# Attention sums and values in four column strips, DMA transposes from the eleventh pair on, and a new division of the first batch, in a fused attention and MLP kernel

## The chip, the cores and the metric

The kernel runs on one core of a Trainium2 chip. The metric is device time in microseconds, the median of the runs shown. Lower is better.

## The reference, cut to what matters

Cosine attention over 8 batches of 12 heads (448 positions, 64 dimensions each), and behind it an MLP with a leaky ReLU on the 3584 tokens that come out.

```
q, k, v: (8, 12, 448, 64) f32, tau = 0.1
q_n = q / (norm(q) + 1e-6);  k_n = k / (norm(k) + 1e-6)
attn = softmax(q_n @ k_n.T / tau)
x = (attn @ v), laid out as (8 * 448, 12 * 64) = (3584, 768)
h = x @ w_in                        # w_in (768, 2048)
out = max(0.01 * h, h) @ w_out      # w_out (2048, 768)
```

## The kernel before, in words

The work is cut into 48 slots, one for each pair of heads (8 batches of 6 pairs, `NSLOT`). A pair's 448 positions lie as 112 partitions of 4 positions (`P`, `T4`). For each pair:

- `load` (L73) brings q, k and v by three DMAs of 224 KB on SP's queue. `squares` (L90, on POOL in the loop), `sums` (L101, DVE), `roots` (L107, ACT: a logarithm and an exponential), `recips` and `normalise` (L111, L120, DVE) make the normalised q and k as bf16 tiles `qn`. `cast_v` (L83, POOL) makes the bf16 v.
- `transposes` (L135) turns `qn` by 8 TensorE transposes into one PSUM tile `tp`, and one copy on DVE brings them to `qkT`, with the 64 dimensions of the two heads on 128 partitions.
- `scores` (L153) makes key-by-query scores for the key blocks that it is given, two of four at a time; each of the two heads takes 64 rows of the array, and ACT takes the exponential of both heads' scores in one instruction (L170), into `pe`. There are two score tiles `sc` in PSUM.
- `values` (L176) sums the exponentials by a matmul with `ones` (`sm`, L181), takes the reciprocal on ACT as Exp(-Ln) (`rb`, L188 and L189), and multiplies with v (`po`, L193). Head 0 has output partitions 0 to 63 and head 1 has 64 to 127: two strips of 64 columns. `scale_out` (L201) multiplies `po` by `rb` on DVE, into `xT`, which holds two batches with the 768 model dimensions on partitions.

The MLP runs in 8 chunks of 384 or 512 tokens (`chunk_cols`). `first` (L217) makes one block of 128 hidden units from 6 matmuls (L223), with a Prelu on ACT (L229) to `hT`. `second` (L233) makes 128 tokens by 384 outputs from 16 matmuls (L237), a copy on DVE (L246) and output DMAs on SP's queue (L257). The tiles `tp`, `sm`, `po` and the MLP's `pm` and `po2` share four PSUM banks (`p_mm`).

The order on each engine is the order in which the program issues (`manual_schedule`). Slot s prepares the squares of s + 3, the sums of s + 2 and the transposes of s + 1. In slots 0 to 6 (`EARLY`) there is attention alone; from slot 7 on, `feed` puts MLP groups between the two halves of the scores and behind the second half, by a credit of `MOE_US` = 6.1 us of estimated TensorE time for each slot. A chunk may start in slot 6(c + 1) + 1. The weights come by DMAs from POOL: four of 768 KB for w_in in slots 1 to 4, two of 1536 KB for w_out in slots 5 and 6. Behind slot 48 the rest of the MLP runs by itself.

Of the kernel before, what the change touches and what calls it, by code (L numbers as in the profile page):

```python
# [8 lines left out]
F32 = mybir.dt.float32  # L9
BF16 = mybir.dt.bfloat16  # L10
AF = mybir.ActivationFunctionType
ALU = mybir.AluOpType
# [4 lines left out]
def kernel(  # L17
# [10 lines left out]
    nc = tc.nc  # L28
    B, H, S, D = q.shape
    N_tok, D_model = out.shape  # L30
    D_ff = moe_w_in.shape[1]
# [6 lines left out]
    NSLOT = B * NPAIR  # L38
    KT = D_model // 128
    MT = D_ff // 128  # L40
    HALF = D_model // 2

# [3 lines left out]
    vbp = ctx.enter_context(tc.tile_pool(name="vb", bufs=4))  # L46
# [3 lines left out]
    qtp = ctx.enter_context(tc.tile_pool(name="qt", bufs=2))  # L50
    pep = ctx.enter_context(tc.tile_pool(name="pe", bufs=2))
# [8 lines left out]
    nc.scalar.preload_act_table_set("natural_log_exp_and_others")  # L60
    w_in_sb = cpool.tile([128, KT, D_ff], BF16, name="w_in_sb")
    w_out_sb = cpool.tile([128, MT, D_model], BF16, name="w_out_sb")
    w_in_r = moe_w_in.rearrange("(ko ki) n -> ki ko n", ki=128)
    w_out_r = moe_w_out.rearrange("(mo mi) n -> mi mo n", mi=128)


    def heads(x, s, n):
        b, h0 = s // NPAIR, 2 * (s % NPAIR)
        return x[b, h0 : h0 + 2 * n].rearrange("h (p t) d -> p h t d", t=T4)
# [3 lines left out]
    def load(s, engs=(nc.sync, nc.sync)):  # L73
        raw[s] = []
        for x, eng, name in zip((q, k), engs, ("q_h", "k_h")):
            t = ldp.tile([P, 2, T4, D], F32, name=name)
            eng.dma_start(out=t, in_=heads(x, s, 1))
            raw[s].append(t)
        t = ldp.tile([P, 2, T4, D], F32, name="v_h")
        nc.sync.dma_start(out=t, in_=heads(v, s, 1))  # L80
        vf[s] = t

    def cast_v(s, eng):  # L83
        t = vbp.tile([P, 2, T4, D], BF16, name="v_b")
        eng.tensor_copy(out=t, in_=vf[s])  # L85
        vh[s] = t
# [3 lines left out]
    def squares(s, engs):  # L90
        tiles = []
        for x, eng in zip(raw[s], engs):
            sq = sqp.tile([P, 2, T4, D], F32, name="sq")
            if eng is nc.scalar:
                nc.scalar.activation(sq, x, func=AF.Square)
            else:
                eng.tensor_tensor(sq, x, x, op=ALU.mult)  # L97
            tiles.append(sq)
        sqs[s] = tiles

    def sums(s):  # L101
        x = smp.tile([P, 2, 2, T4], F32, name="ss")
        for i, sq in enumerate(sqs[s]):
            nc.vector.tensor_reduce(x[:, i], sq, axis=AX.X, op=ALU.add)  # L104
        ss[s] = x

    def roots(s):  # L107
        nc.scalar.activation(ss[s], ss[s], func=AF.Ln, bias=tiny)
        nc.scalar.activation(ss[s], ss[s], func=AF.Exp, scale=0.5)

    def recips(s):  # L111

        r = smp.tile([P, 2, 2, T4], F32, name="r")
        nc.vector.tensor_scalar_add(ss[s], ss[s], 1e-6)
        nc.vector.reciprocal(r, ss[s])
        rn[s] = r

    qn = {}

    def normalise(s):  # L120
        pair = []
        for i, x in enumerate(raw[s]):
            t = qnp.tile([P, T4, 2, D], BF16, name=f"qn{i}")
            nc.vector.tensor_tensor(  # L124
                t,
                x.rearrange("p h t d -> p t h d"),
                rn[s][:, i].rearrange("p h t -> p t h").unsqueeze(3).to_broadcast([P, T4, 2, D]),
                op=ALU.mult,
            )
            pair.append(t)  # L130
        qn[s] = pair
# [3 lines left out]
    def transposes(s, copy=nc.vector.tensor_copy):  # L135
        tp = mmp.tile([128, 2, T4, P], BF16, name="tp", tag="mm")
        for i in range(2):
            for t in range(T4):
                nc.tensor.matmul(  # L139
                    out=tp[:, i, t, :],  # L140
                    lhsT=qn[s][i][:, t].rearrange("p h d -> p (h d)"),
                    rhs=id128[:P, :P],
                    is_transpose=True,
                    start=(i == 0 and t == 0),
                    stop=(i == 1 and t == T4 - 1),
                )
        dst = qtp.tile([128, 2, S], BF16, name="qkT")
        copy(out=dst, in_=tp.rearrange("p i t c -> p i (t c)"))  # L148
        qkT[s] = dst
# [3 lines left out]
    def scores(s, kis):  # L153
        if s not in pe:
            pe[s] = pep.tile([P, T4, 2, S], BF16, name="pe")
# [18 lines left out]
    xT, rbs, pos = {}, {}, {}  # L174

    def values(s):  # L176

        sm = mmp.tile([128, 512], F32, name="sm", tag="mm")
        for ki in range(T4):
            for a in range(2):  # L180
                nc.tensor.matmul(  # L181
                    out=sm[64 * a : 64 * a + 64, :S],
                    lhsT=ones,
                    rhs=pe[s][:, ki, a, :],
                    start=(ki == 0), stop=(ki == T4 - 1),
                )
        rb = rbp.tile([128, S], F32, name="rb")
        nc.scalar.activation(rb, sm[:, :S], func=AF.Ln)  # L188
        nc.scalar.activation(rb, rb, func=AF.Exp, scale=-1.0)  # L189
        po = mmp.tile([128, 512], F32, name="po", tag="mm")  # L190
        for ki in range(T4):
            for a in range(2):
                nc.tensor.matmul(  # L193
                    out=po[64 * a : 64 * a + 64, :S],
                    lhsT=vh[s][:, a, ki, :],
                    rhs=pe[s][:, ki, a, :],
                    start=(ki == 0), stop=(ki == T4 - 1),
                )
        rbs[s], pos[s] = rb, po

    def scale_out(s):  # L201
        b, j = divmod(s, NPAIR)
        m, half = divmod(b, 2)
        if m not in xT:
            xT[m] = xtp.tile([128, NPAIR, 2 * S], BF16, name="xT")
        nc.vector.tensor_tensor(  # L206
            xT[m][:, j, half * S : (half + 1) * S], pos[s][:, :S], rbs[s], op=ALU.mult
        )

# [53 lines left out]

    work = []
    for c in range(B):
        c0, n = chunk_cols(c)
        at = NPAIR * (c + 1) + 1
        for m in range(MT):
            work.append((at, 6 * n / 2400, lambda c=c, m=m: first(c, m)))
        for ts in range(n // 128):  # L270
            for half in range(2):
                work.append((at, 16 * HALF / 2400, lambda c=c, ts=ts, half=half: second(c, ts, half)))
    credit = [0.0]

    def feed(slot, us):
        if not work or work[0][0] > slot:
            return
        credit[0] += us
        while work and work[0][0] <= slot and credit[0] >= work[0][1] / 2:
            at, cost, fn = work.pop(0)  # L280
            fn()
            credit[0] -= cost


    def load_w_in(i):
        n0 = i * (D_ff // 4)
        nc.gpsimd.dma_start(
            out=w_in_sb[:, :, n0 : n0 + D_ff // 4], in_=w_in_r[:, :, n0 : n0 + D_ff // 4]
        )

    def load_w_out(i):
        m0 = i * (MT // 2)
        nc.gpsimd.dma_start(
            out=w_out_sb[:, m0 : m0 + MT // 2], in_=w_out_r[:, m0 : m0 + MT // 2]
        )

    gp = nc.gpsimd
# [6 lines left out]
    ones = cpool.tile([P, 64], BF16, name="ones")  # L304
# [6 lines left out]
    recips(0)  # L311
# [3 lines left out]
    cast_v(0, gp)  # L315
# [3 lines left out]
    recips(1)  # L319
    normalise(1)  # L320

    MOE_US = 6.1
    EARLY = 7
    for s in range(NSLOT + 1):
        if s + 3 < NSLOT:
            squares(s + 3, (gp, gp))
        if s + 1 < NSLOT:
            cast_v(s + 1, gp)
        if 1 <= s <= 4:
            load_w_in(s - 1)  # L330
        if 5 <= s <= 6:
            load_w_out(s - 5)
        if s + 4 < NSLOT:
            load(s + 4)
        if s < NSLOT:
            scores(s, (0, 1))
        if s + 2 < NSLOT:
            sums(s + 2)
        if s < EARLY:
            roots(s + 2)  # L340
            transposes(s + 1)
            recips(s + 2)
            if s >= 1:
                values(s - 1)
            scores(s, (2, 3))
            normalise(s + 2)
            if s >= 1:
                scale_out(s - 1)
        else:
            values(s - 1)  # L350
            scale_out(s - 1)
            if s + 2 < NSLOT:
                roots(s + 2)
                recips(s + 2)
            feed(s, MOE_US / 2)
            if s + 1 < NSLOT:
                transposes(s + 1)
            if s < NSLOT:
                scores(s, (2, 3))
            if s + 2 < NSLOT:  # L360
                normalise(s + 2)
        if s >= EARLY:
            feed(s, MOE_US / 2)
    while work:
        feed(NSLOT + NPAIR, 1e9)
# [35 lines left out]
```

## Time and profile before

| | |
|---|---|
| three runs | 487.48, 489.21, 491.65 us; median 489.21 |
| span of the profiled execution | 488.5 us |
| TensorE matmul (PE) busy | 457.7 us, 94% |
| ScalarE (ACT) busy | 300.8 us, 62% |
| VectorE (DVE) busy | 241.1 us, 49% |
| GpSimd (POOL) busy | 139.2 us, 28% |
| DMA | 50.86 MB, mean 104 GB/s |
| mean granted TensorE clock | 0.990 |

The span is the time from the first to the last instruction of one execution on the core, and the busy times are shares of it. Matmuls are pipelined, so a busy PE is not one at its peak. The slices of a row ("tenths") are 40 equal parts of the span, some 12.2 us each. In a line of a group, the last numbers are busy time and mean length of one instruction, then the idle time before them and what ended most of it. SP is the engine whose queue issues most DMAs.

### The profile page before, as it was taken

The numbers are of one execution on the slowest core, as the hardware profiler recorded it, in microseconds if no ns is written. First come the engines' busy times: TensorE is split into PE (matmuls) and PEld (weight loads), VectorE is DVE, ScalarE is ACT, GpSimd is POOL, SyncE is SP. The second block draws the span as 40 slices with busy tenths as digits, with TensorE's granted clock in tenths as the row PEclk, the third lists the DMA queues.
The fourth block names the chain that finished last, engine by engine and source line by source line (L and its number), as shares of the span: only waits on it lengthen the run. The fifth ranks groups of instructions, "written<-read, shape, count | busy, mean of one in ns | idle before, by whom it ended". The sixth has DMA issues, their size and how long they took to land.

```text
span 488.5 us, 8163 instructions
## 1 busy us (share of the span) xinstructions
PE 457.7 (94%) x3186; PEld 240.2 (49%) x3200; DVE 241.1 (49%) x442; ACT 300.8 (62%) x517; POOL 139.2 (28%) x152
## 2 busy tenths in 40 slices
PE   1777899989999999999999999998999999999996
PEld 0333455534445555554455555554445555554463
DVE  4998534573545753474446454456345654120011
ACT  3788776477774578457765467647874558543400
POOL 2976342053230542054222322143222230000000
PEclk9999899989999999999999999999999999999999
DMA  9999990463213460337103551146221330021022
GB/s 195 218 236 244 239 229 7 120 174 85 63 54 92 118 180 23 86 94 203 56 2 103 165 146 58 44 136 191 68 58 34 105 106 2 0 66 32 1 58 72
DMA packets 44455, 50.86 MB, mean 104 GB/s; under 512 B 3329, under 2 KB 40961, under 8 KB 44417
## 3 DMA queue, kind: packets, MB, share of 16 engines
q1 hardware_dynamic: 38960, 43.82, 33.5%
q0 software_dynamic: 5216, 6.29, 7.3%
q8 instruction: 25, 0.41, 0.4%
q10 hardware_dynamic: 240, 0.23, 0.1%
q14 instruction: 14, 0.11, 0.1%
HBM read 45.61 MB, written 11.01 MB: 116 GB/s over the span
## 4 chain that ended last, share of the span: by engine, by line
PE 88%; DMA 5%; ACT 3%; DVE 2%; issue 1%; POOL 1%; SPq 0%; POOLq 0%
PE pm L223 31%; PE po L237 31%; PE sc L162 9%; PE sm L181 8%; PE po L193 7%; PE tp L139 3%; DMA q_h<-in_q_dram 3%; ACT pe L170 2%; DMA v_h<-in_v_dram 2%; DVE qn L124 1%; DVE ss L104 0%; POOL sq L97 0%; ACT rb L189 0%; ACT rb L188 0%; DVE xT L206 0%
## 5 line engine op out<-in xcount | busy, mean ns | idle before, releaser
L170 ACT ACTIVATE pe<-sc 112x896 bf16<-112x896 f32 x192 | 164.5, 915 | 87.5 <-PE sc L162 86.0
L223 PE MATMUL pm<-xT,w_in_sb 128*128 128x384 bf16 (+1 forms) x754 | 153.3, 355 | 1.2 <-issue 0.7
L237 PE MATMUL po<-w_out_sb,hT 128*128 128x384 bf16 x896 | 153.0, 326 | 0.0
L97 POOL TENSOR_TENSOR sq<-q_h 112x512 f32<-112x512 f32 x45 | 48.9, 1087 | 243.1 <-DMA q_h<-in_q_dram 127.9
L237 PEld LDWEIGHTS <-hT 128*128 128x128 bf16 x896 | 84.5, 98 | 66.7 <-issue 13.6
L223 PEld LDWEIGHTS <-w_in_sb 128*128 128x128 bf16 x768 | 72.3, 98 | 78.8 <-issue 17.2
L229 ACT ACTIVATE hT<-pm 128x384 bf16<-128x384 f32 (+1 forms) x128 | 69.4, 542 | 58.4 <-PE pm L223 57.1
L206 DVE TENSOR_TENSOR xT<-po,rb 128x448 bf16<-128x448 f32 x48 | 29.9, 623 | 109.9 <-ACT rb L189 106.4
L246 DVE COPY osb<-po 128x384 f32<-128x384 f32 x56 | 31.2, 557 | 92.2 <-PE po L237 91.4
L162 PE MATMUL sc<-qkT 64*112 64x448 bf16 x384 | 59.4, 378 | 14.5 <-ACT pe L170 11.2
L104 DVE TENSOR_REDUCE ss<-sq 112x8 f32<-112x512 f32 x96 | 60.9, 675 | 0.0
L97 POOL TENSOR_TENSOR sq<-k_h 112x512 f32<-112x512 f32 x47 | 54.6, 1162 | 15.2 <-DMA k_h<-in_k_dram 12.2
L181 PE MATMUL sm<-pe,ones 112*64 112x448 bf16 x384 | 47.1, 368 | 0.0
L193 PE MATMUL po<-pe,v_b 112*64 112x448 bf16 x384 | 46.6, 366 | 0.0
L148 DVE COPY qkT<-tp 128x896 bf16<-128x896 bf16 x47 | 29.0, 617 | 32.2 <-PE tp L139 32.2
L124 DVE TENSOR_TENSOR qn<-k_h,r 112x512 bf16<-112x512 f32 x48 | 43.7, 911 | 0.0
L139 PE MATMUL tp<-id,qn 112*128 112x112 bf16 x384 | 28.9, 219 | 10.5 <-DVE qn L124 10.4
L162 PEld LDWEIGHTS <-qkT 64*112 64x112 bf16 x384 | 19.0, 126 | 39.7 <-issue 26.8
L124 DVE TENSOR_TENSOR qn<-q_h,r 112x512 bf16<-112x512 f32 x48 | 38.0, 791 | 0.3
L85 POOL CAST v_b<-v_h 112x512 bf16<-112x512 f32 x48 | 33.8, 706 | 3.5 <-issue 3.5
L139 PEld LDWEIGHTS <-qn 112*128 112x128 bf16 x384 | 23.9, 100 | 19.9 <-DVE qn L124 11.9
L193 PEld LDWEIGHTS <-v_b 112*64 112x64 bf16 x384 | 22.6, 114 | 15.9 <-issue 1.9
(21 smaller groups left out, 132.7 us busy)
## 6 DMA issues: line engine op xcount, KB each, us to landing
q_h<-in_q_dram SPq DMA_DIRECT2D x48, 224.0 KB, 4.1
v_h<-in_v_dram SPq DMA_DIRECT2D x48, 224.0 KB, 4.5
k_h<-in_k_dram SPq DMA_DIRECT2D x47, 224.0 KB, 4.5
w_in_sb<-in_moe_w_in_dram POOLq DMA_DIRECT2D x4, 768.0 KB, 13.2
w_out_sb<-in_moe_w_out_dram POOLq DMA_DIRECT2D x2, 1536.0 KB, 22.1
out_dram<-osb SPq DMA_DIRECT2D x7, 336.0 KB, 2.8
out_dram<-osb SPq DMA_DIRECT2D x8, 288.0 KB, 2.8
out_dram<-osb SPq DMA_DIRECT2D x8, 240.0 KB, 3.0
```

What stands on the lines that cost most here:

```text
L85: eng.tensor_copy(out=t, in_=vf[s])
L97: eng.tensor_tensor(sq, x, x, op=ALU.mult)
L104: nc.vector.tensor_reduce(x[:, i], sq, axis=AX.X, op=ALU.add)
L124: nc.vector.tensor_tensor(t, x.rearrange("p h t d -> p t h d"), rn[s][:, i].rearrange("p h t -> p t h").unsqueeze(3).to_broadcast([P, T4, ...
L139: nc.tensor.matmul(out=tp[:, i, t, :], lhsT=qn[s][i][:, t].rearrange("p h d -> p (h d)"), rhs=id128[:P, :P], is_transpose=True, start=(i = ...
L162: nc.tensor.matmul(out=sc[:, a, :S], lhsT=x[rows, 1, ki * P : (ki + 1) * P], rhs=x[rows, 0, :], start=True, stop=True,)
L170: nc.scalar.activation(out=pe[s][:, ki], in_=sc[:, :, :S], func=AF.Exp, scale=inv_tau)
L181: nc.tensor.matmul(out=sm[64 * a : 64 * a + 64, :S], lhsT=ones, rhs=pe[s][:, ki, a, :], start=(ki == 0), stop=(ki == T4 - 1),)
L193: nc.tensor.matmul(out=po[64 * a : 64 * a + 64, :S], lhsT=vh[s][:, a, ki, :], rhs=pe[s][:, ki, a, :], start=(ki == 0), stop=(ki == T4 - 1),)
L223: nc.tensor.matmul(out=pm[:, :n], lhsT=w_in_sb[:, kt, m * 128 : (m + 1) * 128], rhs=xT[c // 2][:, kt, c0 : c0 + n], start=(kt == 0), stop= ...
L229: nc.scalar.activation(out=hT[c][:, m, :n], in_=pm[:, :n], func=AF.Prelu, alpha=0.01)
L237: nc.tensor.matmul(out=po2[:, :HALF], lhsT=hT[c][:, m, ts * 128 : (ts + 1) * 128], rhs=w_out_sb[:, m, half * HALF : (half + 1) * HALF], st ...
```

## The change

- **Four strips.** `values` now takes two pairs (a quad) in every second slot. Each of the four heads has a strip of 32 columns. The sums take 4 x 4 matmuls with 32 columns of `ones`. The values of a head are 64 dimensions, so they are made in two passes of 32 each: `cast_v` puts the even and the odd dimensions apart, pass `e` takes the one or the other, and `xT` holds them so, for which w_in's rows are loaded in the matching order. `scale_out` is in `values` now: one multiply per pass, with one `rb` for the quad.
- **Transposes.** From slot 10 on (`DMA_FROM`), q and k are transposed by two DMAs on SP's queue from `qn` straight to `qkT`. For this, sums, roots and normalise run three slots ahead instead of two, and the pools grow: `qkT` 5 buffers, `pe` 3, `v_b` 6.
- **First batch.** Slots 0 to 5 have a loop of their own: k is normalised on POOL, w_in comes by 12 DMAs in slots 0 to 3, w_out by two in slots 4 and 5, cut by output columns instead of by rows. The MLP may start in slot 6. Slot 6 prepares slots 8 and 9 both.
- **MLP groups.** In place of the credit, each group has a place, a slot number with a fraction by its share of TensorE time, spread over 6.3 slots for each chunk; `feed` issues all groups whose place has come.

The diff, cut to its core:

```diff
-    vbp = ctx.enter_context(tc.tile_pool(name="vb", bufs=4))
+    vbp = ctx.enter_context(tc.tile_pool(name="vb", bufs=6))
-    qtp = ctx.enter_context(tc.tile_pool(name="qt", bufs=2))
-    pep = ctx.enter_context(tc.tile_pool(name="pe", bufs=2))
+    qtp = ctx.enter_context(tc.tile_pool(name="qt", bufs=5))
+    pep = ctx.enter_context(tc.tile_pool(name="pe", bufs=3))
...
-    w_in_r = moe_w_in.rearrange("(ko ki) n -> ki ko n", ki=128)
+    w_in_r = moe_w_in.rearrange("(j p e) n -> j p e n", p=128, e=2)
...
+    def load_w_in(i):
+        n0 = i * (D_ff // 4)
+        for j in range(NQ):
+            gp.dma_start(
+                out=w_in_sb[:, 2 * j : 2 * j + 2, n0 : n0 + D_ff // 4],
+                in_=w_in_r[j, :, :, n0 : n0 + D_ff // 4],
+            )
+    def load_w_out(half):
+        n0 = half * HALF
+        gp.dma_start(out=w_out_sb[:, :, n0 : n0 + HALF], in_=w_out_r[:, :, n0 : n0 + HALF])
...
+        t = vbp.tile([P, 2, T4, 2, D // 2], BF16, name="v_b")
+        gp.tensor_copy(
+            out=t.rearrange("p h t e d -> p (h t) e d"),
+            in_=vf[s].rearrange("p h t (d e) -> p (h t) e d", e=2),
+        )
...
+    def normalise(s, k_eng=nc.vector):
...
+        for i, (x, eng) in enumerate(zip(raw[s], (nc.vector, k_eng))):
             t = qnp.tile([P, T4, 2, D], BF16, name=f"qn{i}")
-            nc.vector.tensor_tensor(
+            eng.tensor_tensor(
...
     def transposes(s, copy=nc.vector.tensor_copy):
+        dst = qtp.tile([128, 2, T4, P], BF16, name="qkT")
+        qkT[s] = dst.rearrange("p i t c -> p i (t c)")
+        if s >= DMA_FROM:
+            for i in range(2):
+                nc.sync.dma_start(
+                    out=dst[:, i], in_=qn[s][i].rearrange("p t h d -> p (t h d)"), transpose=True
+                )
+            return
...
+    def values(j):
+        strips = [(2 * j + g // 2, g % 2, slice(32 * g, 32 * g + 32)) for g in range(4)]
+        def strip_products(x, weights):
+            for ki in range(T4):
+                for s, a, rows in strips:
+                    nc.tensor.matmul(
+                        out=x[rows, :S],
+                        lhsT=weights(s, a, ki),
+                        rhs=pe[s][:, ki, a, :],
+                        start=(ki == 0), stop=(ki == T4 - 1),
+                    )
         sm = mmp.tile([128, 512], F32, name="sm", tag="mm")
+        strip_products(sm, lambda s, a, ki: ones)
         rb = rbp.tile([128, S], F32, name="rb")
         nc.scalar.activation(rb, sm[:, :S], func=AF.Ln)
         nc.scalar.activation(rb, rb, func=AF.Exp, scale=-1.0)
...
+        for e in range(2):
+            po = mmp.tile([128, 512], F32, name="po", tag="mm")
+            strip_products(po, lambda s, a, ki: vh[s][:, a, ki, e, :])
+            nc.vector.tensor_tensor(
+                xT[m][:, 2 * jj + e, half * S : (half + 1) * S], po[:, :S], rb, op=ALU.mult
+            )
...
+            work.append((NPAIR * (c + 1) + (NPAIR + 0.3) * (done + cost / 2) / total, fn))
...
+    for s in range(NPAIR):
+        squares(s + 3)
+        cast_v(s + 1)
+        load_w_in(s) if s < 4 else load_w_out(s - 4)
+        load(s + 4)
+        scores(s, (0, 1))
+        sums(s + 2)
+        roots(s + 2)
+        transposes(s + 1)
+        if s >= 2 and s % 2 == 0:
+            values(s // 2 - 1)
+        normalise(s + 2, gp)
+        scores(s, (2, 3))
+    sums(NPAIR + 2)
+    for s in range(NPAIR, NSLOT + 1):
+        ahead = (s + 3, s + 2)[s == NPAIR :] if s == NPAIR else (s + 3,)
+        if s == NPAIR:
+            ahead = (s + 2, s + 3)
+        for n in ahead:
+            squares(n + 1)
+            cast_v(n - 1)
+            load(n + 2)
+        if s % 2 == 0:
+            values(s // 2 - 1)
+        scores(s, (0, 1))
+        for n in ahead:
+            if n != NPAIR + 2:
+                sums(n)
+            roots(n)
+            normalise(n)
+            if DMA_FROM <= n < NSLOT:
+                transposes(n)
+        feed(s + 0.5)
+        if s + 1 < DMA_FROM:
+            transposes(s + 1)
+        scores(s, (2, 3))
+        feed(s + 1)
+    feed(1e9)
```

More of the change, by code (lines that the diff above doesn't have):

```diff
@@ L38 @@
     NSLOT = B * NPAIR
+    NQ = NPAIR // 2
     KT = D_model // 128
@@ L41 @@
     HALF = D_model // 2
+    DMA_FROM = 10
     ctx.enter_context(tc.manual_schedule())
@@ L60, with heads @@
     nc.scalar.preload_act_table_set("natural_log_exp_and_others")
+    gp = nc.gpsimd
     w_in_sb = cpool.tile([128, KT, D_ff], BF16, name="w_in_sb")
     w_out_sb = cpool.tile([128, MT, D_model], BF16, name="w_out_sb")
-    w_in_r = moe_w_in.rearrange("(ko ki) n -> ki ko n", ki=128)
+    w_in_r = moe_w_in.rearrange("(j p e) n -> j p e n", p=128, e=2)
     w_out_r = moe_w_out.rearrange("(mo mi) n -> mi mo n", mi=128)
-    def heads(x, s, n):
+    def load_w_in(i):
[8 more added lines that the diff above has]
+        gp.dma_start(out=w_out_sb[:, :, n0 : n0 + HALF], in_=w_out_r[:, :, n0 : n0 + HALF])
+    def heads(x, s):
         b, h0 = s // NPAIR, 2 * (s % NPAIR)
-        return x[b, h0 : h0 + 2 * n].rearrange("h (p t) d -> p h t d", t=T4)
+        return x[b, h0 : h0 + 2].rearrange("h (p t) d -> p h t d", t=T4)
     raw, vf, vh = {}, {}, {}
     def load(s, engs=(nc.sync, nc.sync)):
+        if s >= NSLOT:
+            return
         raw[s] = []
@@ L76, in load, with cast_v, squares @@
             t = ldp.tile([P, 2, T4, D], F32, name=name)
-            eng.dma_start(out=t, in_=heads(x, s, 1))
+            eng.dma_start(out=t, in_=heads(x, s))
             raw[s].append(t)
         t = ldp.tile([P, 2, T4, D], F32, name="v_h")
-        nc.sync.dma_start(out=t, in_=heads(v, s, 1))
+        nc.sync.dma_start(out=t, in_=heads(v, s))
         vf[s] = t
-    def cast_v(s, eng):
-        t = vbp.tile([P, 2, T4, D], BF16, name="v_b")
-        eng.tensor_copy(out=t, in_=vf[s])
+    def cast_v(s):
+        if s >= NSLOT:
+            return
+        t = vbp.tile([P, 2, T4, 2, D // 2], BF16, name="v_b")
[3 more added lines that the diff above has]
+        )
         vh[s] = t
     ss, rn, sqs = {}, {}, {}
-    def squares(s, engs):
+    def squares(s, engs=None):
+        if s >= NSLOT:
+            return
         tiles = []
-        for x, eng in zip(raw[s], engs):
+        for x, eng in zip(raw[s], engs or (gp, gp)):
             sq = sqp.tile([P, 2, T4, D], F32, name="sq")
@@ L101, in sums @@
     def sums(s):
+        if s >= NSLOT:
+            return
         x = smp.tile([P, 2, 2, T4], F32, name="ss")
@@ L107, in roots @@
     def roots(s):
+        if s >= NSLOT:
+            return
         nc.scalar.activation(ss[s], ss[s], func=AF.Ln, bias=tiny)
         nc.scalar.activation(ss[s], ss[s], func=AF.Exp, scale=0.5)
-    def recips(s):
+    qn = {}
+    def normalise(s, k_eng=nc.vector):
+        if s >= NSLOT:
+            return
         r = smp.tile([P, 2, 2, T4], F32, name="r")
@@ L115, in recips @@
         nc.vector.reciprocal(r, ss[s])
-        rn[s] = r
-    qn = {}
-    def normalise(s):
         pair = []
-        for i, x in enumerate(raw[s]):
+        for i, (x, eng) in enumerate(zip(raw[s], (nc.vector, k_eng))):
             t = qnp.tile([P, T4, 2, D], BF16, name=f"qn{i}")
-            nc.vector.tensor_tensor(
+            eng.tensor_tensor(
                 t,
                 x.rearrange("p h t d -> p t h d"),
-                rn[s][:, i].rearrange("p h t -> p t h").unsqueeze(3).to_broadcast([P, T4, 2, D]),
+                r[:, i].rearrange("p h t -> p t h").unsqueeze(3).to_broadcast([P, T4, 2, D]),
                 op=ALU.mult,
@@ L135, in transposes @@
     def transposes(s, copy=nc.vector.tensor_copy):
+        dst = qtp.tile([128, 2, T4, P], BF16, name="qkT")
[5 more added lines that the diff above has]
+                )
+            return
         tp = mmp.tile([128, 2, T4, P], BF16, name="tp", tag="mm")
@@ L146, in transposes @@
                 )
-        dst = qtp.tile([128, 2, S], BF16, name="qkT")
-        copy(out=dst, in_=tp.rearrange("p i t c -> p i (t c)"))
-        qkT[s] = dst
+        copy(out=dst, in_=tp)
     pe = {}
     def scores(s, kis):
+        if s >= NSLOT:
+            return
         if s not in pe:
@@ L172, in scores @@
             )
-    xT, rbs, pos = {}, {}, {}
-    def values(s):
-        sm = mmp.tile([128, 512], F32, name="sm", tag="mm")
[L179 to L186, printed above, removed]
+    xT = {}
+    def values(j):
[9 more added lines that the diff above has]
+                    )
+        sm = mmp.tile([128, 512], F32, name="sm", tag="mm")
+        strip_products(sm, lambda s, a, ki: ones)
         rb = rbp.tile([128, S], F32, name="rb")
@@ L189, in values @@
         nc.scalar.activation(rb, rb, func=AF.Exp, scale=-1.0)
[L190 to L202, printed above, removed]
+        b, jj = divmod(j, NQ)
         m, half = divmod(b, 2)
         if m not in xT:
[L205 to L208, printed above, removed]
+            xT[m] = xtp.tile([128, KT, 2 * S], BF16, name="xT")
+        for e in range(2):
[4 more added lines that the diff above has]
+            )
     hT = {}
@@ L266, with feed @@
         c0, n = chunk_cols(c)
[L267 to L297, printed above, removed]
+        groups = [(6 * n, lambda c=c, m=m: first(c, m)) for m in range(MT)]
+        order = [(ts, half) for half in range(2) for ts in range(n // 128)] if c == 0 else [
+            (ts, half) for ts in range(n // 128) for half in range(2)
+        ]
+        groups += [
+            (MT * HALF, lambda c=c, ts=ts, half=half: second(c, ts, half)) for ts, half in order
+        ]
+        total, done = sum(g[0] for g in groups), 0
+        for cost, fn in groups:
+            work.append((NPAIR * (c + 1) + (NPAIR + 0.3) * (done + cost / 2) / total, fn))
+            done += cost
+    def feed(place):
+        while work and work[0][0] <= place:
+            work.pop(0)[1]()
     load(0, (nc.sync, nc.scalar))
@@ L303 @@
     nc.vector.memset(tiny, 1e-18)
-    ones = cpool.tile([P, 64], BF16, name="ones")
+    ones = cpool.tile([P, 32], BF16, name="ones")
     nc.vector.memset(ones, 1.0)
@@ L310 @@
     roots(0)
-    recips(0)
     normalise(0)
@@ L314 @@
     squares(2, (nc.scalar, gp))
-    cast_v(0, gp)
+    cast_v(0)
     transposes(0, nc.scalar.copy)
@@ L318 @@
     roots(1)
[L319 to L340, printed above, removed]
-            transposes(s + 1)
[L342 to L363, printed above, removed]
@@ L364 @@
-    while work:
-        feed(NSLOT + NPAIR, 1e9)
+    normalise(1, gp)
+    for s in range(NPAIR):
[32 more added lines that the diff above has]
+        if s + 1 < DMA_FROM:
+            transposes(s + 1)
+        scores(s, (2, 3))
+        feed(s + 1)
```

## The prediction

> **What bounds the kernel now.** I read the page first (busy shares, slices, chain), then the windows, then the timeline of one slot in the middle. A slot is one turn of the main loop, that is one pair of heads. The page:
>
> ```profile
> PE 457.7 (94%) x3186; PEld 240.2 (49%) x3200; DVE 241.1 (49%) x442; ACT 300.8 (62%) x517; POOL 139.2 (28%) x152
> PE   1777899989999999999999999998999999999996
> DMA  9999990463213460337103551146221330021022
> PE 88%; DMA 5%; ACT 3%; DVE 2%; issue 1%; POOL 1%; SPq 0%; POOLq 0%
> ```
>
> PE carries 88% of the chain that ended last, and its row is at 9 from the fifth slice on. Only the first four slices (49 us) are something else: DMA is full there, and PE is not. So a matmul removed after about 54 us shortens the kernel by its time on PE; one removed before is worth nothing by itself. The chain in order of time gives the two borders, the first and the last block of pm (L223):
>
> ```profile
> 53.97 3.80 PE pm L223 x18
> ...
> 442.67 10.74 PE pm L223 x49
> ```
>
> Between them lie 41 slots (7 to 47) in 388.7 us, 9.48 us a slot. What one slot costs on PE I take from the timeline (start, length, engine, line):
>
> ```profile
> 253.99 0.56 PEld L139 LDWEIGHTS <-qn 112*128 112x128 bf16 x8
> 254.64 0.58 PE L162 MATMUL sc<-qkT 64*112 64x448 bf16 x4
> ...
> 258.38 0.95 PE L181 MATMUL sm<-pe,ones 112*64 112x448 bf16 x8
> ...
> 259.16 0.92 PE L193 MATMUL po<-pe,v_b 112*64 112x448 bf16 x8
> ...
> 260.02 2.29 PE L237 MATMUL po<-w_out_sb,hT 128*128 128x384 bf16 x13
> ```
>
> From the first transpose to the next matmul that isn't one: 254.64 - 253.99 = 0.65 us for 8 transposes. From sm's start to po's: 0.78 us for 8 matmuls, so 0.195 us for two. They stand in two strips of 64 columns and run together, since one alone streams 448 columns, as long as the scores do. From sm's start to L237 it is 1.64 us; 8 twos at 0.195 make 1.56, and the rest, 0.08 us, is the change of the array's layout.
>
> **The sum, part by part.** It is made against the span of the profiled execution, 488.5 us; the median of the three runs is 489.21, and 0.7 between them is less than their spread (487.48 to 491.65).
>
> 1. **Strips.** Two pairs now take 16 twos for sums and values, 16 x 0.195 = 3.12 us, and two changes of layout, 0.16. After, two pairs take 16 sum matmuls and 32 value matmuls (32 output columns each, so a head's values need two), in fours: 12 fours. No row shows four strips. The lower bound of a four is that of a two, 0.195, if four overlap as two do; the upper one is 0.39, if only two ever overlap. I take 0.195: the two strips show no loss from sharing (0.195 is all that one needs), and their weight loads lie beside the matmuls. So 12 x 0.195 + 0.08 = 2.42 against 3.28: 0.86 us a quad. Of the 24 quads 20.5 lie behind 53.97: **-17.6 us**. ACT computes Ln and Exp (rb) once for four heads and not twice.
>
> The Trainium skill (TensorE: Matmul & The Clock Gate, section "Measured speedup vs the span model") gives 2.38 times for three column strips and 3.07 times for four row strips, less than the full factor. By 3.07, a four would be an estimated 0.254 us and the total some 15 us higher; the trace's twos show no such loss, and no row here shows fours.
>
> 2. **Transposes.** From slot 10 on, 38 slots lose 8 PE transposes, 38 x 0.65 = **-24.7 us**, and a DVE copy each (0.617 us, off the path). In their place come 76 DMAs on SP's queue, each 112 x 512 bf16 = 114.7 KB. They are issued three slots ahead with five qkT buffers, so some 20 us of latency hide; what counts is whether the DMA engines have the room. In the windows:
>
> ```profile
> 12.00:24.00 12.00, 8.61 (x50) 3.68 (x47) 11.49 (x18) 8.96 (x16) 11.44 (x12) 1.00 1.14 218
> 24.00:36.00 12.00, 8.31 (x76) 4.54 (x77) 11.68 (x20) 10.90 (x18) 8.36 (x11) 0.96 1.20 235
> 36.00:48.00 12.00, 9.50 (x80) 4.67 (x78) 10.70 (x18) 10.04 (x18) 8.79 (x9) 0.90 1.17 245
> ...
> 240.00:280.00 40.00, 39.89 (x291) 21.04 (x290) 20.35 (x39) 24.43 (x41) 10.24 (x12) 1.00 0.29 84
> 280.00:320.00 40.00, 40.00 (x296) 22.19 (x294) 19.04 (x39) 27.47 (x52) 9.31 (x12) 1.00 0.31 89
> ```
>
> (columns: PE, PEld, DVE, ACT, POOL busy, PE clock, DMA share, GB/s). Over the six 40 us windows from 160 to 400 the DMA share averages 0.352 at 99 GB/s, so a full share would be 282 GB/s, and a slot uses 3.3 of its 9.48 us. The new slot is 9.48 - 0.65 - 0.43 = 8.40 us, which leaves 5.1 us, or **2.5 us for each transposing DMA**. No row shows one. Lower bound: the bytes at the full rate, 114.7 / 282 = 0.41 us. Upper: a load of 224 KB lands 4.1 to 4.5 us after its issue; if a transpose held all the engines for 4.5 us, two would need 9. I take 1 us, by the bytes and twice more for short pieces: hidden, cost 0. The cover is the idle 5.1 us; without it every us per DMA costs 2 x 38 = 76 us.
>
> The skill's pages disagree here. VectorE: DVE Perf Modes, section "The three transpose paths", puts a 128x128 bf16 block at 1309 ns through the DMA crossbar and advises TensorE where PSUM will do; four such blocks one after the other would be an estimated 5.2 us for each DMA, and the kernel far slower than before. DMA: Bandwidth & Descriptors, section "Latency and other measured facts", has 261 GB/s, an estimated 0.44 us, and hides it all. No run here shows either.
>
> On SP each pair of transposes waits for qn of its own slot (DVE); behind it stand the outputs of this slot and the loads of the next, which POOL's squares need a slot later. I put that at 0: loads land in 4.5 us, a slot is 8.4.
>
> 3. **The first batch.** In 12 to 48 us DVE is busy 33.9 of 36 us: it sets the pace, 5.5 us a slot (exp starts 12.4 for slot 0, 50.9 for slot 7). The change gives POOL the k half of normalise (911 ns on DVE). But POOL is busy 28.6 of these 36 us, 4.4 a slot, and gets per slot one more multiply (nearest row: its squares, 1.09 to 1.16 us, say 1.2) and, in slots 0 to 3, three weight DMAs for one, 2 x 0.9 = 1.8 us (w_in issue 915 ns). So POOL needs 7.4 us in four slots and 5.6 in two. MLP work (L223) starts in slot 6 rather than 7, after six slots. If POOL sets the pace, from 13.4 us (the first squares of the loop): 4 x 7.4 + 5.6 = 35.2 until qn of slot 6, then scores, two exps, values: first pm near 54.5. If ACT does (5.3 us a slot less half of rb, 4.7), near 46.5. I take 51, **-3 us**. Slot 6 then has about **+1.5 us** of scores left behind that start.
>
> 4. **Joints.** In slot 6 two pairs are prepared at once, and ACT waits in order for roots of slot 9, whose load came only a slot earlier and took 7 us; the MLP's Prelus stand behind it and PE's four mm banks run out. **+4 us**, between 0 and 8. In the long stage ACT is busy 156 of 240 us, 6.2 a slot, less 0.56 for rb: 5.6 of 8.4. DVE 5.0 - 0.6, POOL 3.0 (the cast reads every second element, still far from full). None takes over, but the waits inside a slot (values: sm, rb, xT, all in ACT's and DVE's order) get less cover: **+5 us**, between 0 and 10. Spreading the MLP by place costs nothing on a full PE. The last chunk (41 us of pure PE) stays.
>
> Sum: 488.5 - 17.6 - 24.7 - 3 + 1.5 + 4 + 5 = **453.7 us**; I say 453.
>
> **Rivals.**
>
> - **DMA becomes the bound** (slower). Place: SP's queue from slot 10. Against it: share 0.35 today. For it: no row has a transposing transfer, and this one writes 128 partitions in pieces of 224 bytes. Every us above 2.5 per DMA costs 76 us; it decides from 2.5 + 35/76 = 3.0 us. At the upper bound 4.5 us a slot takes 12.3 us: 453 + 3.9 x 38 = 601 us. Chance 0.11.
> - **Four strips overlap only two at a time.** Then the values cost more than before: 12 x 0.195 x 20.5 = 48 us more, 501 us. It decides from a four of 0.34 us. For it: four moving streams at once are shown nowhere; against: the twos. Chance 0.05; that a four costs 0.25 to 0.3, giving 467 to 479, 0.08.
> - **POOL sets the first batch.** First pm at 59 instead of 51, from multiplies stretched by DVE (squares run 1.03 to 1.57 us there): 461 us. For it POOL's 11.44 of 12 us in the second window. Chance 0.13.
>
> **Numbers.** The forecast has 0.60 (its own range 443 to 463), a wash 0.03. Faster by over 1% (1% is 4.9 us, about what a measurement of this kernel can tell): 0.60 + 0.13 + 0.08 + part of the wash = 0.82. Slower: 0.11 + 0.05 - a little = 0.14; within: 0.04. The range goes from 440 (no joints, early start) to 482 (fours at 0.3 us, or DMAs at 2.9).
>
> **What would show it.** Right: L139 and L148 with 10 slots' worth; sm matmuls starting in fours 0.19 us apart; first pm near 51; slots of 8.4 us; DMA share near 0.5 to 0.6 in the middle, and scores not waiting for a DMA. Wrong: scores of slot 10 and on released by qkT's DMA; po and sm stretched beyond 0.3 us a four; the first pm after 56; PE under 9 in the middle.

## The result and the profile after

The changed kernel takes 463.93 us (median of four runs, 463.74 to 465.03) against 488.75 us on the same chip: a ratio of 0.9505, interval 0.9467 to 0.9543. The forecast was 453 in a range of 440 to 482. The profiled execution took 464.04 us with a span of 462.2, so 26.3 us less than the 488.5 of before, where the sum had 34.8.

The page after, the lines that answer to those shown of before (busy shares, slices, chain by engine):

```profile
PE 426.7 (92%) x3280; PEld 211.6 (46%) x3280; DVE 225.6 (49%) x397; ACT 277.6 (60%) x469; POOL 156.2 (34%) x167
PE   0577869989999999989999999989999999989996
POOL 1987952323242224253422344244332330000000
DMA  9999993648335644665445644665345531111022
PE 85%; DVE 3%; DMA 3%; ACT 3%; POOL 3%; issue 1%; SPq 0%; POOLq 0%
```

PE is still the bound from about 64 us on. DMA, at 0 to 7 tenths in the middle before, is now at 3 to 6 there. POOL is at 7 to 9 in the first batch. `pm` is the PSUM tile of the MLP's first half, and its first matmuls mark the end of the first batch. The two borders, the first pm from the timeline and the last chunk from the chain:

```profile
54.43 3.10 PE L254 MATMUL pm<-xT,w_in_sb 128*128 128x384 bf16 x18
```

```profile
416.55 20.72 PE pm L254 x96
```

Before they stood at 53.9 (53.97 in the chain) and 442.67. So the first batch is worth nothing (0.5 us later, with one slot less done), and nearly all of the 26.3 us lie between the borders: 388.8 us before, 362.1 after. Over twelve slots in the middle (exponentials of slots 12 to 24) a slot takes 8.62 us; the prediction had 8.40. One values block of the timeline after:

```profile
260.81 0.94 PE L219 MATMUL sm<-pe,ones 112*32 112x448 bf16 x16
261.58 1.69 PE L219 MATMUL po<-pe,v_b 112*32 112x448 bf16 x32
263.20 0.59 PE L198 MATMUL sc<-qkT 64*112 64x448 bf16 x4
```

A four is a group of four matmuls, one for each strip. 16 sum matmuls take 0.77 us, four fours at 0.19, and 32 value matmuls 1.62 us, eight fours at 0.19 and 0.1 for the change of layout: 2.39 us for a quad, 2.42 in the prediction. In the trace the four of a group start within 10 ns of one another, as the twos did.

Adding up starts between the borders gives where the 26.7 us come from: sums and values 63.5 us before and 48.2 after; transposes 15.7 and 1.2; scores 37.9 and 41.4; the pauses between kinds 20.4 and 21.2; MLP 251.4 and 250.2. (Some records are missing, so these are good to a microsecond.)

### The profile page after: what moved, and what is told of

It reads as the page before. It is cut to its first block, busy times and chain, and to the rows that moved or that the text cites. A ratio compares the mean times of both kernels' runs of the same rounds, so it can differ in the third digit from the quotient of the medians.

```text
span 462.2 us, 8433 instructions
## 1 busy us (share of the span) xinstructions
PE 426.7 (92%) x3280; PEld 211.6 (46%) x3280; DVE 225.6 (49%) x397; ACT 277.6 (60%) x469; POOL 156.2 (34%) x167
## 4 chain that ended last, share of the span: by engine, by line
PE 85%; DVE 3%; DMA 3%; ACT 3%; POOL 3%; issue 1%; SPq 0%; POOLq 0%
PE po L268 32%; PE pm L254 30%; PE sc L198 9%; PE po L219 9%; PE sm L219 5%; ACT pe L206 3%; DMA k_h<-in_k_dram 2%; DVE qn L152 2%; DMA v_h<-in_v_dram 2%; POOL w_in_sb L75 1%; POOL sq L123 1%; POOL qn L152 1%; DVE ss L132 1%; DVE ss L147 0%; PE tp L175 0%
## 5 line engine op out<-in xcount | busy, mean ns | idle before, releaser
L206 ACT ACTIVATE pe<-sc 112x896 bf16<-112x896 f32 x192 | 164.5, 914 | 63.5 <-PE sc L198 63.4
L123 POOL TENSOR_TENSOR sq<-q_h 112x512 f32<-112x512 f32 x45 | 51.1, 1137 | 201.0 <-DMA q_h<-in_q_dram 119.7
L198 PE MATMUL sc<-qkT 64*112 64x448 bf16 x384 | 62.1, 390 | 13.7 <-ACT pe L206 10.3
L123 POOL TENSOR_TENSOR sq<-k_h 112x512 f32<-112x512 f32 x47 | 55.2, 1174 | 12.4 <-DMA k_h<-in_k_dram 12.4
L238 DVE TENSOR_TENSOR xT<-po,rb 128x448 bf16<-128x448 f32 x48 | 28.0, 620 | 57.2 <-ACT rb L230 50.4
L147 DVE TENSOR_SCALAR ss<-ss 112x16 f32<-112x16 f32 x48 | 16.9, 351 | 73.5 <-ACT ss L139 73.4
L219 PE MATMUL po<-pe,v_b 112*32 112x448 bf16 x768 | 44.2, 374 | 0.0
L152 DVE TENSOR_TENSOR qn<-k_h,r 112x512 bf16<-112x512 f32 x41 | 40.7, 992 | 0.0
L229 ACT ACTIVATE rb<-sm 128x448 f32<-128x448 f32 x24 | 13.0, 543 | 37.9 <-PE sm L219 37.9
L219 PEld LDWEIGHTS <-v_b 112*32 112x32 bf16 x768 | 21.6, 102 | 18.1 <-issue 4.0
L219 PE MATMUL sm<-pe,ones 112*32 112x448 bf16 x384 | 25.3, 382 | 0.1
L175 PE MATMUL tp<-id,qn 112*128 112x112 bf16 x80 | 8.4, 254 | 14.7 <-DVE qn L152 9.1
```

The source lines that it names most:

```text
L152: eng.tensor_tensor(t, x.rearrange("p h t d -> p t h d"), r[:, i].rearrange("p h t -> p t h").unsqueeze(3).to_broadcast([P, T4, 2, D]), op ...
L198: nc.tensor.matmul(out=sc[:, a, :S], lhsT=x[rows, 1, ki * P : (ki + 1) * P], rhs=x[rows, 0, :], start=True, stop=True,)
L206: nc.scalar.activation(out=pe[s][:, ki], in_=sc[:, :, :S], func=AF.Exp, scale=inv_tau)
L219: nc.tensor.matmul(out=x[rows, :S], lhsT=weights(s, a, ki), rhs=pe[s][:, ki, a, :], start=(ki == 0), stop=(ki == T4 - 1),)
L238: nc.vector.tensor_tensor(xT[m][:, 2 * jj + e, half * S : (half + 1) * S], po[:, :S], rb, op=ALU.mult)
```

## The experiments

Times are medians; the changed kernel is at 463.93.

**The transposes alone.** The edit, with `e4_early` (below) as the partner:

```diff
-    DMA_FROM = 10
+    DMA_FROM = NSLOT
```

> The changed kernel with all 48 slots transposed on TensorE, and the transposes of slot s + 1 set ahead of the preparation of slot s + 3, so that their copy does not stand behind it on DVE (e4_early has that order with the DMA transposes). To be compared with e4_early: the difference is what the 38 slots of DMA transposes are worth. Theory A: it is their matmul time alone, start to start in the trace of before: 15.71 us for 280 starts in 40 slots, 0.056 us each, 8 of them 0.45 us a slot, 17 us for 38 slots; so some 17 us over e4_early. Rival B, the prediction's term: 0.65 us a slot, 25 us over e4_early. Rival C: the DVE copy of 0.62 us counts too, over 30 us.

Measured: 477.74 us, 14.0 over `e4_early` (463.70), or 0.37 us a slot. Rivals B and C fall; A is near, 3 us too high. (Its 15.71 us are those of all 320 transposes in the 40 slots, 0.39 a slot, so its own term makes 15 us.) The twelve slots take 107.7 us here and 103.4 with the DMA, 0.36 a slot. The starts show the parts: 0.40 a slot for the transposes and 0.05 of pauses fall away, and 0.08 comes back on the scores, whose starts take 10.7 us in twelve slots with the transposes on PE and 11.7 without. PE, freed of transposes, comes to the scores sooner and waits there for ACT's exponentials.

**The strips alone.**

```diff
-            for ki in range(T4):
-                for s, a, rows in strips:
-                    nc.tensor.matmul(
-                        out=x[rows, :S],
...
+                for ki in range(T4):
+                    for a in range(2):
+                        nc.tensor.matmul(
+                            out=x[64 * a : 64 * a + 64, :S],
...
```

> The changed kernel with sums and values in two strips of 64 columns again, two pairs one after the other, with v and w_in's rows in the old order; all else stays. Theory A: a four takes what a two takes (0.19 us), so the quad costs 16 twos and not 12 fours, and one more rb on ACT: +0.76 us for 21 quads behind the first pm, 16 us over the changed kernel, 480 us, a little more if ACT's second rb (1.1 us a quad) holds PE up. Rival B: four strips brought nothing because fours are slower than they look by their starts: under 5 us.

Measured: 481.86 us, 17.9 more. Theory A: 16.0 of them are the sums and values themselves, whose starts take 64.1 us between the borders against 48.1, 0.76 a quad. The other 1.9 lie in slots 6 to 8 (slot 6 takes 12.4 us, not 10.3); that they are ACT's second rb isn't shown. Four strips run as four.

**Do the DMA engines have room?**

```diff
+            extra = xqp.tile([128, 2, T4, P], BF16, name="extra")
             for i in range(2):
-                nc.sync.dma_start(
-                    out=dst[:, i], in_=qn[s][i].rearrange("p t h d -> p (t h d)"), transpose=True
-                )
+                for d in (extra, dst):
+                    nc.sync.dma_start(
+                        out=d[:, i], in_=qn[s][i].rearrange("p t h d -> p (t h d)"), transpose=True
+                    )
```

> The changed kernel with every DMA transpose made twice, the first into a tile that nobody reads: 152 in place of 76. Theory A: the DMA engines have the room (share 0.53 in the middle, some 0.6 us for one transpose) and SP too (1.2 us of issue each): time within 1.5 us of 463.9, share near 0.67. Rival B: the transposes cost already by sharing the engines with the loads; then the second lot makes POOL's squares and the scores wait: 4 us or more.

Measured: 463.81 us, the same. In the windows (columns as in the prediction; DMA share and GB/s last) the changed kernel and this one:

```profile
240.00:280.00 40.00, 40.00 (x348) 21.04 (x348) 20.99 (x36) 24.68 (x42) 16.00 (x15) 1.00 0.55 141
```

```profile
240.00:280.00 40.00, 40.00 (x348) 20.96 (x346) 17.75 (x37) 24.66 (x42) 12.94 (x15) 1.00 0.88 180
```

and the changed kernel's transposes among its DMA issues (from issue to landing, us):

```profile
qkT<-qn SPq DMA_TRANSPOSE x76, 2.4
```

Over the five 40 us windows from 160 to 360 us the share is 0.356 before, 0.532 after and 0.748 with the transposes doubled. With slots of 9.5, 8.62 and 8.62 us that is 3.4, 4.6 and 6.4 us of the engines a slot, so one transpose takes 0.6 us of them, and each of the added ones 0.9. Theory A, though its share of 0.67 was low.

**The first batch, four edits.** What stands in slot 2, from the timeline of the changed kernel:

```profile
23.11 2.18 POOL L75 DMA_DIRECT2D w_in_sb<-in_moe_w_in_dram  x3
25.31 1.06 POOL L152 TENSOR_TENSOR qn<-k_h,r 112x512 bf16<-112x512 f32 x1
26.43 0.55 PE L175 MATMUL tp<-id,qn 112*128 112x112 bf16 x4 [1.74 <-POOL qn L152]
26.91 1.68 PE L219 MATMUL sm<-pe,ones 112*32 112x448 bf16 x16
28.38 3.20 PE L219 MATMUL po<-pe,v_b 112*32 112x448 bf16 x32
31.51 0.91 PE L198 MATMUL sc<-qkT 64*112 64x448 bf16 x4
32.18 3.34 ACT L206 ACTIVATE pe<-sc 112x896 bf16<-112x896 f32 x4 [2.38 <-PE sc L198]
```

Three things in a row: POOL issues weight DMAs and k's multiply waits for them; the transposes wait for k; the sums and values then take 4.6 us (0.37 us a four, half the pace of later) ahead of the second scores, and ACT stands. The edit for the last of these:

```diff
-        if s >= 2 and s % 2 == 0:
-            values(s // 2 - 1)
         normalise(s + 2, gp)
         scores(s, (2, 3))
+        if s >= 2 and s % 2 == 0:
+            values(s // 2 - 1)
```

> The changed kernel with values in slots 2 and 4 of the first batch behind the second half of the scores, not ahead of it. Theory A: in slots 2 and 4 ACT stands for some 5 us while the sums and values run on PE at half pace (0.37 us a four), because the second scores stand behind them; then the first pm comes about 4 to 7 us earlier than 54.4 and the time falls to 457 to 460. Rival B: POOL's order (squares, cast, three weight DMAs, k's multiply) sets the pace of every slot, and PE's order is only where the wait shows: under 1.5 us gain.

Measured: 460.06 us, first pm at 50.1. That is 3.9 us, the lower end of theory A. Next, the k half of the multiply back on DVE:

```diff
-        normalise(s + 2, gp)
+        normalise(s + 2)
```

> The changed kernel with k normalised on DVE in the first batch, as before. Theory A: POOL's line (squares 2.06, cast 0.62, weight DMAs 2.2, k's multiply 1.06 to 1.5 us) sets the first batch, and the transposes wait for k's multiply behind the weight DMAs (some 2 us in slots 1 and 2); DVE is free half of the time there (5.6 to 6.2 of 12 us). So the first pm comes 2 to 5 us earlier than 54.4, time 459 to 462. Rival B: PE's order and its half pace set the batch, and moving k changes under 1 us. Rival C: DVE is full again, as in the kernel before: 2 us or more slower.

Measured: 461.86 us, 2.1 less, and first pm at 53.2, 1.2 earlier: theory A by the time, under its 2 to 5 us by the first pm. The part of the change that moved k to POOL costs 2 us as it stands. Third, the weight DMAs behind k's multiply on POOL:

```diff
-        load_w_in(s) if s < 4 else load_w_out(s - 4)
...
         normalise(s + 2, gp)
+        load_w_in(s) if s < 4 else load_w_out(s - 4)
```

> The changed kernel with the weight DMAs of each slot of the first batch issued on POOL behind k's multiply, not ahead of it. Theory A: the transposes of slots 2 to 4 no longer wait for the 2.2 us in which POOL issues three DMAs; first pm 2 to 4 us earlier, time 460 to 462. Rival B: POOL's sum stays what it is and the wait only moves to the squares of the next slot: under 1 us.

Measured: 464.34 us, no gain, as rival B has it, but not by its mechanism. The first pm came 1.8 us earlier (52.6), nearly as theory A has it, and slot 6 then lasted 12.2 us in place of 10.3: ACT waited 4.88 us for the sums of slot 9 (3.86 in the changed kernel), and PE then ran at half pace for a stretch (last section). Fourth, the two that helped, together:

> The changed kernel with two changes to the first batch: the values behind the second scores (e3_values_late, 3.9 us less) and k normalised on DVE (e5_k_on_dve, 2.1 us less). Theory A: they stand at different waits (ACT for the second scores, PE for k) and add: 457 to 459. Rival B: with the values late, k's wait is hidden, or DVE is full: 460 or more.

Measured: 460.78 us, rival B: they don't add. The window from 24 to 36 us says why (the third and fifth busy columns are DVE and POOL):

```profile
24.00:36.00 12.00, 9.56 (x80) 4.00 (x80) 11.68 (x16) 8.06 (x15) 11.93 (x14) 1.00 1.18 240
```

DVE is at 11.68 of 12 and POOL at 11.93. With k on DVE the first batch is as full there as it was in the kernel before, and POOL stays full with squares, casts and weight DMAs.

**The half pace.** On top of `e10_late_and_dve`:

```diff
+    def spare(s, count):
+        x = mmp.tile([128, 512], F32, name="spare", tag="mm")
+        for _ in range(count):
+            nc.tensor.matmul(out=x[:, :S], lhsT=id128, rhs=qkT[s][:, 0, :], start=True, stop=True)
...
+        spare(s, 6)
         transposes(s + 1)
...
         scores(s, (2, 3))
+        spare(s, 6)
```

> As e10_late_and_dve, with twelve spare matmuls of 448 columns in each slot of the first batch (six ahead of the transposes, six behind the second scores) whose result nobody reads. Theory A: PE's half pace there (0.37 us a four against 0.19 later) comes from too little work on PE; the spare work, 2.2 us a slot at full pace, brings the fours of slots 2 and 4 to 0.19, and the first pm comes 1 to 3 us earlier. Rival B: the pace doubles but POOL and the loads set the batch: within 1 us of e10_late_and_dve. Rival C: PE stays at half pace and the spare matmuls cost their 4.5 us a slot: 10 us or more slower.

Measured: 459.72 us against 460.78, whose runs overlap with these, and the first pm stayed at 51.1. The pace did double; the values of slot 2 here:

```profile
29.84 0.94 PE L219 MATMUL sm<-pe,ones 112*32 112x448 bf16 x16
30.61 1.69 PE L219 MATMUL po<-pe,v_b 112*32 112x448 bf16 x32
```

The clock column from 36 to 48 us reads 1.00 here and 0.72 in `e10_late_and_dve`. So too little work on PE is what halves its pace there, and rival B holds: the pace doesn't set the batch.

**Slot 6.** Between 56 and 64 us PE loses some 4 us. First idea, the copy of qkT behind a later slot's preparation:

```diff
         scores(s, (0, 1))
+        if s + 1 < DMA_FROM:
+            transposes(s + 1)
         for n in ahead:
...
-        if s + 1 < DMA_FROM:
-            transposes(s + 1)
         scores(s, (2, 3))
```

> The changed kernel with the TensorE transposes of slots 7, 8 and 9 set ahead of the preparation of slot s + 3 (and 8) in slots 6 to 8. Theory A: between 56 and 64 us PE waits because the copy of qkT for slot 7 stands on DVE behind sums, roots and normalise of slots 8 and 9; PE loses about 4 us there and another 0.5 to 1 at 79: time falls by 3 to 5 us. Rival B: ACT's Prelus behind the roots of slot 9 are what stops PE (four PSUM banks full from 58.4 to 61.4), and those stay: gain under 1.5 us.

Measured: 463.70 us, no gain; rival B. Slot 7 did begin 1.2 us earlier (63.45 against 64.62), but 0.9 of it was lost in that slot, where the clock column reads 0.76 and 0.81 from 60 to 68 us and 1.00 in the changed kernel. Its timeline of ACT shows the wait that stayed:

```profile
59.54 0.31 ACT L138 ACTIVATE ss<-ss,tiny 112x16 f32<-112x16 f32 x1 [3.86 <-DVE ss L132]
59.88 0.21 ACT L139 ACTIVATE ss<-ss 112x16 f32<-112x16 f32 x1
60.00 1.23 ACT L260 ACTIVATE hT<-pm 128x384 bf16<-128x384 f32 x3
```

ACT waits 3.86 us, in order, for the sums of slot 9, and the three Prelus that would free PE's banks come behind. The next kernel moved that preparation behind the second scores, with the late values and late weight DMAs:

```diff
+        prepare(ahead[0])
         feed(s + 0.5)
         if s + 1 < DMA_FROM:
             transposes(s + 1)
         scores(s, (2, 3))
+        for n in ahead[1:]:
+            prepare(n)
```

> The changed kernel with the late values of e3_values_late, the late weight DMAs of e6_weights_late, and slot 6's second preparation (roots and normalise of slot 9) behind the second scores. Theory A for the last part: in slot 6 ACT waits 3.9 us for the sums of slot 9 with three Prelus behind it, and PE stops because its four banks are full (e4_early showed that it isn't the copy); without it PE loses 3 us less. Sum: 3.9 for the values, 0 to 3 for the weights, 3 for slot 6: 454 to 457. Rival B: the parts hide one another, 459 to 460 as e3_values_late alone.

Measured: 458.66 us, the fastest of all, but only 1.4 under `e3_values_late`. The first pm came at 49.1, 1.0 earlier, so little is left for slot 6. Part of the 1.4 can be the clock (last section). The wait of slot 6 was not removed but put off: ACT waits 2.98 us for sums at 57.8 and 1.53 at 62.3, and pm waits 2.06 us for a Prelu at 63.3. Rival B is nearer.

**Two more.** DMA transposes from slot 8 on, on top of `e10_late_and_dve`:

```diff
-    DMA_FROM = 10
+    DMA_FROM = 8
```

> As e10_late_and_dve, with DMA transposes from slot 8 on in place of 10. Theory A: the copies of slots 8 and 9 on DVE and 0.9 us of PE fall away, and a copy no longer waits behind a later slot's preparation: 1 to 2 us less than e10_late_and_dve. Rival B: the DMA engines are full until some 70 us (share over 1 in the windows), the transposes of slot 8 land late or hold up the loads: no gain or slower.

Measured: 460.68 us, no gain; rival B. In the window from 60 to 72 us the DMA share went from 0.99 to 1.33. But neither late transposes nor late loads ate the microsecond: in the profiled execution slot 10 begins 0.8 us earlier than in `e10_late_and_dve` (85.69 against 86.53) and slot 47 still does (402.21 against 403.06). Of this 0.7 is lost behind the last matmul, where the last output ends 4.9 us later instead of 4.2. A gain of this size is below what four runs can tell. And the spare matmuls on `e7_together`:

> As e7_together (k on POOL, values late, weight DMAs late), with the spare matmuls of e11_spare_matmuls. Theory A: in e11_spare_matmuls the full pace brought nothing because DVE and POOL were both full (11.5 to 12 of 12 us); here DVE has room, and the values of slots 2 and 4 (4.6 us at half pace, 2.3 at full) stand ahead of the next slot's scores, for which ACT waits. So the first pm comes 1.5 to 3 us earlier than 49.1 and the time falls to 455 to 457. Rival B: POOL alone (5.9 us in slots 0 to 3) sets the batch here too: within 1 us of 458.7.

Measured: 459.16 us; rival B. The first pm came 0.8 us earlier (48.4) and slot 7 then took 12.2 us, with ACT waiting 2.97 us for sums there and the clock column at 0.86 and 0.71 from 60 to 68 us. POOL in the window from 24 to 36:

```profile
24.00:36.00 12.00, 10.59 (x104) 5.05 (x104) 8.06 (x15) 8.96 (x14) 11.96 (x15) 1.00 1.18 231
```

With PE at full pace and DVE at 8.06 of 12, POOL alone is full (11.96), and stays so to 48 us. By this busy share it is the floor of this first batch, as it is divided here; no run with POOL relieved and DVE free was made.

## Why the prediction was right or wrong

- **What bounds the kernel: right.** PE's matmuls behind the first pm were what the change could save, and nearly all of the gain came from there. (PE's row is at 8 in the fifth slice, and at 9 from the sixth on but for the ninth.)
- **Strips, -17.6: right.** A quad takes 2.39 us for the predicted 2.42, and without the strips the kernel is 17.9 us slower, 16.0 of it in the sums and values. The lower bound of a four, a two's own time, was the one to take. The page TensorE: Matmul & The Clock Gate of the Trainium skill ("Measured speedup vs the span model") has less than the full factor for packed tiles; here the factor is full in a running stream.
- **Transposes on PE, -24.7: the mis-sized term.** It measured 14.0. The step took 0.65 us from the weight load's row (253.99) to the next kind of matmul. The matmul rows of the kernel before show it shorter:

```profile
254.15 0.56 PE L139 MATMUL tp<-id,qn 112*128 112x112 bf16 x8
254.64 0.58 PE L162 MATMUL sc<-qkT 64*112 64x448 bf16 x4
```

That is 0.49 us. The first weight load lay beside the matmuls ahead of it, and 0.1 us of the 0.49 is the change of layout to the scores, which stays, since the MLP's matmuls now stand there. So 0.39 a slot was there by the kernel before, 15 us, and 0.45 with the pauses by `e1_pe_transposes`, 17 us at most; 0.08 a slot came back as waits of the scores for ACT.
- **DMA hidden: right.** A transpose takes 0.6 us of the engines, between the bounds of 0.41 and 4.5 and under the 1 us taken, and twice as many cost nothing. Of the two pages of the Trainium skill that were weighed, DMA: Bandwidth & Descriptors is the nearer with its estimated 0.44 us; four blocks at 1.3 us one after the other, from VectorE: DVE Perf Modes, are not what a 112 x 512 transpose costs here (2.4 us from issue to landing). The latter's advice for TensorE would have cost 14 us here.
- **First batch, -3: wrong, +0.5 measured.** The upper bound, first pm near 54.5 if POOL sets the pace, has the number (54.43) by luck. POOL's line was put at 7.4 us a slot; squares 2.06, cast 0.62, weight DMAs 2.2 and k's multiply 1.06 make 5.9. And the working left out PE at half pace, with the values ahead of the second scores: `e3_values_late` takes 3.9 us off by order alone, and only then is POOL's line the floor, near 48 to 49.
- **Slot 6, +4: right, mechanism and size.** ACT's wait of 3.86 us for slot 9's sums is the one named; the pauses around pm between 54 and 104 us exceed their usual 0.1 by 4.0 us, 3.1 of them behind the Prelus and 0.9 for the copy of qkT on DVE. That ACT's order could be mended for 3 us was not borne out.
- **Waits in the long stage, +5: too large, and at another place.** Over slots 14 to 46 the scores' starts take 32.0 us against 29.5 before, 2.5 more, or some 3 us over 41 slots. PE waits there for ACT's exponentials; between sums and values, where the prediction looked, there is no pause. In `e1_pe_transposes` the same slots take 30.1, so most of this wait came with the transposes' removal.

The two terms that were most off, by 10.7 and 3.5 us, would make it 467.9 from 453.7; the span is 462.2. Of the +5 only some 3 us were there, and 2 to 3 of these are in the 14.0 already. That accounts for 4 to 5 us of the difference; the rest, about 1 us, stays open. So 463.93 us lies just above the forecast's own 443 to 463.

## What to carry to other kernels

Price a removed matmul from the start of its own row to the start of the next kind, without the weight load that lies beside earlier work and without the layout change that will stay. On this PE-bound stage, narrow outputs packed in four strips paid in full, and transposes moved to DMA engines with room paid 0.37 of the 0.45 us a slot that they took. In a start-up stage where several engines are near full, adding up one engine's line gives a floor at best; look also at what stands ahead of what in PE's order.

## What the runs showed that was not expected

In the first batch PE ran at half pace (a four in 0.37 us). The clock column (third from the end) shows it in one window and not in the other:

```profile
24.00:36.00 12.00, 8.74 (x78) 3.79 (x77) 5.63 (x12) 6.47 (x13) 10.23 (x12) 0.98 1.20 238
36.00:48.00 12.00, 8.58 (x70) 3.42 (x67) 6.15 (x11) 6.83 (x11) 9.27 (x12) 0.59 1.15 225
```

The values of slot 4, from 40.6 us on, ran under a clock of 0.50 (36 to 44 us). Those of slot 2, from 26.9 us on, lie ahead of this trace's first clock record at 32.2 us, and the column counts time without a record as full. There the starts of matmuls, and not the column, show the pace.

No idle stretch of PE from 24 to 36 us is longer than about 2 us, and from 32 to 36, just before the clock falls, none is longer than 0.7. The Trainium skill (TensorE: Matmul & The Clock Gate, section "Why this matters for your kernels") warns of idle gaps over some 3 us. Here shorter ones went with the half pace, and 2.2 us of spare matmuls a slot brought the full pace back.

The half pace can return in slot 6, behind PE's wait for the Prelus. The changed kernel and `e6_weights_late`:

```profile
61.36 2.11 PE L254 MATMUL pm<-xT,w_in_sb 128*128 128x384 bf16 x12 [2.92 <-ACT hT L260]
```

```profile
60.60 3.78 PE L254 MATMUL pm<-xT,w_in_sb 128*128 128x384 bf16 x12 [3.94 <-ACT hT L260]
```

The same twelve matmuls take 1.7 us more, with the clock column at 0.58 from 60 to 64 us. In `e3_values_late` and `e10_late_and_dve` they take 3.7 us as well; in `e7_together` the twelve behind that wait, in slot 7 there, take 2.11. So differences of 1 to 2 us between these kernels, as the 1.4 of `e7_together` under `e3_values_late`, can't be put down to the edit alone.
